# Attention and a Fourier mix on one core: another outermost dimension for two kinds of transfer, and new figures for transfers in the planner

## The chip, the cores and the metric

The kernel runs on one core of a Trainium2 chip. A core has five engines with queues of their own: TensorE (PE, matmuls; its weight loads are shown apart as PEld), VectorE (DVE), ScalarE (ACT), GpSimd (POOL) and SyncE (SP), which here issues every transfer. Sixteen DMA engines move the data. The metric is the device time of one execution in microseconds (us), the median of the runs. All data is float32 and the matmuls take it in the float32r form.

## The reference

Two results stand side by side in the output of 2048 x 2048: attention with 32 heads of 32 channels, and the real part of a two-dimensional Fourier transform made with given matrices.

```python
H = 32; Dh = D // H                       # B, S, D = 1, 2048, 1024
q, k, v = split(x @ wqkv)                 # each (B, H, S, Dh)
scores = einsum("bhqd,bhkd->bhqk", q, k) * Dh ** -0.5
p = softmax(scores, axis=-1)
o = einsum("bhqk,bhkd->bhqd", p, v)
a = o.transpose(0, 2, 1, 3).reshape(B, S, D) @ wo

re = einsum("bsd,ed->bse", x, dft_hid_re)
im = einsum("bsd,ed->bse", x, dft_hid_im)
b = einsum("ts,bse->bte", dft_seq_re, re) - einsum("ts,bse->bte", dft_seq_im, im)
return concatenate([a, b], axis=-1)
```

## The kernel before, in words

**Dense products.** The projections to queries, keys and values (`qkv`), the two Fourier stages (`dense1`, `dense2`) and the output projection (`project`) are done with a scheme of seven products of half-size blocks, whose sums and differences are formed by `fetch` (line 389) on DVE or POOL. Each operand is split into a high and a low part (`halves`, lines 409 to 414), and three matmuls (high x high, low x high, high x low) make one product; line 325 issues them. The text calls these matmuls the fills. Intermediate tensors live in DRAM: `qk_d` for queries and keys, `v_d` for values, `u_d` for partial sums of the seven products, `o_d` for the heads' results, `r_d` for the inverse row sums. Loads of kept partial sums are `c<-u_d` (line 636), and line 557 or 559 adds the result of a group of matmuls to them. In the steps that load and store many `u_d`, from about 540 to 810 us, the queries, keys and values of the later blocks are made.

**Attention** runs beside the fills, head by head. `scores` (line 1062) makes the scores in rows of queries, 1024 keys at a time; DVE takes the maximum (line 1068), ACT the exponentials and their row sums (line 1071). Then `transposed` makes the scores again with keys on the partitions and with the maximum as two more rows of the product (line 1193), so that ACT's exponential (line 1197) is the numerator itself. Line 1211 multiplies it with the values, and lines 1222 and 1224 gather the result in a tile `ot`. Its 128 partitions are 4 groups of 512 queries times 32 channels.

**Row sums.** `sums(h)` turns the row sums of head h, takes the inverse, stores it to `r_d[h]` (8 KB, line 1161) and loads it back into `rt` (line 1154), each group's 512 values onto its 32 partitions. `result(h)` multiplies `ot` with `rt` (line 1239) and stores it to `o_d[h // 4]` (line 1241). `project` reads `o_d` back as operands of 128 rows, four heads times 32 channels for one group of queries, when the heads are done.

**Order.** The program is written out by a planner. Each operation is an `Op` with an engine, a cost in us, what it waits for and a rank; `Plan` keeps a clock for each engine and starts an operation when its engine is free and its inputs are there. PE takes its work from three streams of attention and the list of fills. Some element-wise operations go to POOL or DVE, whichever the plan finds free. Operations of SP cost `ISSUE` each; a transfer of `kb` ends when the bytes ahead of it have moved at `KB_US` = 340 KB per us, and `LANDING` = 1.8 us later; SP begins one only if the plan's backlog of bytes is at most `QUEUE` = 1.0 us. What the plan decides is the fixed order of each engine's instructions. The times at which they run are the chip's.

Of the kernel before, what the change touches and what calls it, by code (L numbers as in the profile page):

```python
# [9 lines left out]
F32 = mybir.dt.float32  # L10
# [7 lines left out]
P = 128  # L18
S = 2048
D = 1024  # L20
H = 32
DH = 32
NC = D // P
NS = S // P
NB = 512
# [9 lines left out]
class Op:  # L35


    __slots__ = ("engine", "cost", "emit", "rank", "kb", "other", "left", "ready", "end", "begun", "then", "soon")

    def __init__(self, engine, cost, emit, rank=0.0, kb=0, other=None):  # L40
        self.engine, self.cost, self.emit, self.rank, self.kb, self.other = engine, cost, emit, rank, kb, other
        self.left, self.ready, self.end, self.begun = 0, -1e3, None, False
        self.then, self.soon = [], []


# [15 lines left out]
class Plan:  # L61
# [13 lines left out]
    def __init__(self):  # L75
        self.now = 0.0
        self.free = {e: 0.0 for e in ("PE", "ACT", "DVE", "POOL", "SP")}
        self.pending = {e: [] for e in ("ACT", "DVE", "POOL", "SP")}
        self.able = {e: [] for e in ("ACT", "DVE", "POOL", "SP")}
        self.dma = 0.0  # L80
        self.seq = 0

    def op(self, engine, cost, emit, after=(), uses=(), rank=0.0, kb=0, order=None, other=None):

        o = Op(engine, cost, emit, rank, kb, other)
        seen = set()
        for d in after:
            if d is not None and id(d) not in seen:  # L90
                seen.add(id(d))
                self._wait(o, d)
        for u in uses:
            u.append(o)
        if order is not None:
            p, order.first = order.first, o
            if p is not None and not p.begun:
                p.soon.append(o)
                o.left += 1
        if o.left == 0:  # L100
            self._release(o)
        return o
# [18 lines left out]
    def start(self, o, e=None):  # L121
        e = e or o.engine
        o.emit(e) if o.other else o.emit()
        o.begun = True
        self.free[e] = self.now + (o.cost if e == o.engine else o.other[1])
        if o.kb:
            self.dma = max(self.dma, self.free[e]) + o.kb / self.KB_US
            o.end = self.dma + self.LANDING
        else:
            o.end = self.free[e]  # L130
            self.free[e] -= self.OVERLAP.get(e, 0.0)
        for t in o.then:
            t.ready = max(t.ready, self.after(o, e, t))
            t.left -= 1
            if t.left == 0:
                self._release(t)
        for t in o.soon:
            t.ready = max(t.ready, self.now)
            t.left -= 1
            if t.left == 0:  # L140
                self._release(t)
        o.then = o.soon = ()
        o.emit = None
# [28 lines left out]

    def begin(self, e):

        return self.free[e] if e != "SP" else max(self.free[e], self.dma - self.QUEUE)


@with_exitstack
def kernel(
# [11 lines left out]
    nc = tc.nc  # L191

    dram = ctx.enter_context(tc.tile_pool(name="dram", bufs=1, space=DRAM))
# [4 lines left out]
    v_d = [dram.tile([P, 16, NS, DH], F32, name=f"v_d{b}") for b in range(2)]  # L198
    r_d = [dram.tile([NS, P], F32, name=f"r_d{h}") for h in range(H)]

    o_d = [dram.tile([4, P, NB], F32, name=f"o_d{c}") for c in range(NC)]
    ab_d = [[[dram.tile([P, NB], F32, name=f"ab_d{m}_{e}_{k}") for k in range(NS)] for e in range(2)] for m in range(2)]
    s1_d = [dram.tile([P, 4, P], F32, name=f"s1_d{i}") for i in range(8)]
    t1_d = [dram.tile([P, NB], F32, name=f"t1_d{n}") for n in range(8)]
# [69 lines left out]
    ES, ET = 1.22, 0.61  # L274
    MAX, EVAC, CAST, BIT = 1.22, 0.69, 0.45, 0.27
    SUB = 1.34
    ISSUE = 0.36

    LATE = 0.3
    HB = 0  # L280
# [13 lines left out]
    op = pl.op  # L294
# [639 lines left out]
    def project():  # L934


        def q_a(r, k, j, c):
            return o_d[4 * k + c][2 * r + j], [o for h in range(4) for o in o_st[16 * k + 4 * c + h]]

        def a_terms(p, j, c):  # L940
            q = lambda r, k: q_a(r, k, j, c)
            return {
                1: lambda: [(1, *q(0, 0))], 2: lambda: [(1, *q(0, 1))], 4: lambda: [(1, A22[j][c])],
                5: lambda: [(1, A22[j][c]), (1, *q(1, 0))],
                6: lambda: [(1, A22[j][c]), (-1, S2[j][c])],
                7: lambda: [(1, *q(0, 0)), (-1, *q(1, 0))],
                3: lambda: [(1, *q(0, 1)), (-1, S2[j][c])],
            }[p]()

        def b_terms(p, c):  # L950
            q = lambda k, e: wo[4 * k + c, :, e * NB : e * NB + NB]
            return {
                1: lambda: [(1, q(0, 0), [])], 2: lambda: [(1, q(1, 0), [])], 3: lambda: [(1, q(1, 1), [])],
                5: lambda: [(1, q(0, 1), []), (-1, q(0, 0), [])],
                6: lambda: [(1, T2[c]), (1, q(0, 0), [])],
                7: lambda: [(1, q(1, 1), []), (-1, q(0, 1), [])],
                4: lambda: [(1, T2[c]), (-1, q(1, 0), [])],
            }[p]()


        WHERE = {
            1: ([16, 20], 0), 7: ([8, 12], 24), 2: ([0, 8], 20), 6: ([12, 0], 24),
            5: ([8, 12], 20), 3: ([0, 8], 24), 4: ([12, 0], 20),
        }
        A, B, X, Y = {}, {}, {}, {}

        def kept(name):
            box = {}

            def get():  # L970
                if "t" not in box:
                    box["t"] = op_pool().tile([P, NB], F32, name=name)
                return box["t"]

            return Kept(get)

        A22 = [[kept(f"a22_{j}_{c}") for c in range(4)] for j in range(2)]
        S2 = [[kept(f"s2_{j}_{c}") for c in range(4)] for j in range(2)]
        T2 = [kept(f"t2_{c}") for c in range(4)]

        def load_b(p):
            for c in range(4):
                B[p, c] = moving(WHERE[p][1] + c, b_terms(p, c), None, T2[c] if p in (6, 7) else None)

        def load_a(p, which):
            for j, c in which:
                if p == 6:
                    fetch([P, NB], [(1, *q_a(1, 1, j, c))], None, A22[j][c])
                A[p, j, c] = moving(WHERE[p][0][j] + c, a_terms(p, j, c), None, S2[j][c] if p in (6, 7) else None)

        J0, J1 = ([(j, c) for c in range(4)] for j in range(2))
        ORDER = (1, 7, 2, 6, 5, 3, 4)
        tail, where[0] = where[0], within
        load_b(1)
        load_a(1, J0 + J1)
        where[0] = tail
        for x, p in enumerate(ORDER):
            for i in range(8):
                j, t = divmod(i, 4)
                if p == 1 and i % 2 == 0:  # L1000
                    X[i // 2] = accs(4 + i // 2)
                if p == 7 and i % 2 == 0:
                    Y[i // 2] = accs(16 + i // 2)
                h = DONE.get(p)
                to = out[(8 * h[0] + i) * P : (8 * h[0] + i) * P + P, h[1] * NB : h[1] * NB + NB] if h else None
                xi, yi = X[i // 2][i % 2], Y[i // 2][i % 2] if Y else None

                group(((((A[p, j, c]), lambda u, t=t: u[:, t * P : t * P + P]), (B[p, c], whole)) for c in range(4)), 4,
                      gather(1, yi, None, None, None, None) if p == 7 else gather(p, xi, yi, None, to, []))
                if p == 6:  # L1010
                    yi.last = add_op(
                        lambda e, xi=xi, yi=yi: (nc.gpsimd if e == "POOL" else nc.vector).tensor_tensor(out=yi.at(), in0=xi.at(), in1=yi.at(), op=ALU.add),
                        [xi.last, yi.last], [xi.users, yi.users], seq())
                if x < 6 and i == 3:
                    n = ORDER[x + 1]
                    load_b(n)
                    if n != 7:
                        load_a(n, J0)
                if x == i == 0:
                    load_a(7, J0 + J1)  # L1020
                if x < 6 and i == 7 and ORDER[x + 1] != 7:
                    load_a(ORDER[x + 1], J1)
# [97 lines left out]
    def sums(h):  # L1120
# [29 lines left out]

        def spread():
            rt[h] = att().tile([P, NB], F32, name="rt", bufs=1)
            r = r_d[h].rearrange("(j a) b -> j (a b)", j=4).rearrange("j (o n) -> j o n", o=1)
            nc.sync.dma_start(rt[h], r.broadcast_to([4, DH, NB]))

        a = op("DVE", 2 * BIT, sub, exps + told, [tuse, suse, nuse], -2)
        b = op("ACT", BIT, ex, [a], [tuse], -2)
# [2 lines left out]
        d = op("DVE", BIT, copy, [m, *sold], [users, srs], -2)  # L1160
        e = op("SP", ISSUE, lambda: nc.sync.dma_start(r_d[h], box["s"]), [d], [srs], -2, 8)
        rold, ruse = rt_r.take()
        g = op("SP", ISSUE, spread, [e, *rold], [ruse], -2, 256)
        rts[h] = (g, ruse)
        return m

# [69 lines left out]
    def result(h, e, po, ouse):  # L1236
# [1 line left out]
        a = add_op(  # L1238
            lambda e: (nc.gpsimd if e == "POOL" else nc.vector).tensor_tensor(out=po["o"], in0=po["o"], in1=rt[h], op=ALU.mult),
            [e, load], [ouse, ruse], -1)  # L1240
        o_st[h].append(op("SP", ISSUE, lambda: nc.sync.dma_start(o_d[h // 4][:, h % 4 * DH : h % 4 * DH + DH, :], po["o"]), [a], [ouse], -2, 256))

    qkv()
    for w in (1, 0):
# [137 lines left out]
```

## Time and profile before

| | |
|---|---|
| median of three runs | 3128.91 us (3128.57 to 3138.54) |
| profiled execution | 3130.3 us, its span 3128.5 us |
| PE busy | 3065.6 us, 98% of the span |
| DVE, ACT, POOL busy | 2501.8, 2305.5, 888.0 us |
| moved by DMA | 567.76 MB, 181 GB/s in the mean |
| mean granted clock of TensorE | 0.995 |

The span is the time from the first to the last instruction of the profiled execution; the execution's own time has 1.8 us more around it. Lines such as "L1241 SPq DMA_DIRECT2D o_d<-ot" name the line of the kernel, the engine's queue, the operation and what it writes and reads. "SPq" is SP's sequencer, the time it needs to issue a transfer. The granted clock is a share of full speed; at 0.5 a matmul takes twice as long.

### The profile page before, as it was taken

To read this page: it belongs to the slowest core of one execution; us is meant where nothing else is said; L and a number is where in the kernel's file an instruction comes from. 1 tells how busy PE (TensorE), PEld (TensorE's weight loads), DVE (VectorE), ACT (ScalarE), POOL (GpSimd) and SP (SyncE) were. 2 spreads that over 40 slices of the span, in tenths; PEclk is the share of its full clock that TensorE was granted. 3 is DMA by queue.
4 is the path that set the end of the run, shared out by engine and by line. 5 is a ranking of instruction groups with operands and counts; after the bars stand their busy time and mean duration, and the time that the engine had idled before them with its cause. 6 is when DMAs were issued, how large, how long until landed. Compare 5 with 4: busy or idle time off the path is not lost.

```text
span 3128.5 us, 45280 instructions
## 1 busy us (share of the span) xinstructions
PE 3065.6 (98%) x15040; PEld 2146.0 (69%) x15040; DVE 2501.8 (80%) x3206; ACT 2305.5 (74%) x4316; POOL 888.0 (28%) x659
## 2 busy tenths in 40 slices
PE   9899999999999999999999999999999999999999
PEld 7687666566666666666666666666666666666787
DVE  7669889977777877787777888888777888887886
ACT  4237888777888888888888887888888878775321
POOL 3423323401102222221001244233211235333453
PEclk9999999999999999999999999999999999999999
DMA  9976557876634544464443576545433467456952
GB/s 332 321 239 189 185 166 239 298 225 191 194 94 145 184 142 148 138 190 146 138 126 100 182 228 194 157 146 181 132 116 103 147 215 227 150 156 194 329 177 92
DMA packets 357368, 567.76 MB, mean 181 GB/s; under 512 B 84336, under 2 KB 85872, under 8 KB 357136
## 3 DMA queue, kind: packets, MB, share of 16 engines
q1 hardware_dynamic: 357136, 564.86, 57.0%
q8 instruction: 121, 1.98, 0.3%
q14 instruction: 111, 0.91, 0.1%
HBM read 407.70 MB, written 156.50 MB: 180 GB/s over the span
## 4 chain that ended last, share of the span: by engine, by line
PE 80%; DVE 11%; DMA 5%; issue 2%; ACT 2%; SPq 1%; POOL 0%; DVEq 0%; ACTq 0%; POOLq 0%
PE pd L325 34%; PE psT L1193 13%; PE pd L1211 13%; PE psS L1062 13%; PE psT L325 5%; DVE negm L1068 3%; ACT psS L1071 1%; DVE slot L414 1%; DMA raw<-in_xa 1%; DVE slot L411 1%; DVE raw L389 1%; DVE h L411 1%; DVE l L414 1%; DMA g<-in_ct 1%; DMA c<-u_d 0%
## 5 line engine op out<-in xcount | busy, mean ns | idle before, releaser
L1197 ACT ACTIVATE pt<-psT 128x512 f32<-128x512 f32 x2048 | 1159.5, 629 | 332.6 <-PE psT L1193 327.5
L1068 DVE TENSOR_REDUCE negm<-psS 128x1 f32<-128x1024 f32 x1024 | 1232.7, 1218 | 194.0 <-PE psS L1062 190.0
L1071 ACT ACTIVATE psS<-psS,negm 128x1024 f32<-128x1024 f32 x1024 | 1148.7, 1122 | 175.7 <-DVE negm L1068 169.5
L325 PE MATMUL pd<-slot,h 128*128 128x512 f32 x3336 | 1163.4, 397 | 9.6 <-DVE c L557 6.2
L1193 PE MATMUL psT<-qs,ks 98*128 98x512 f32 x2048 | 822.7, 405 | 2.3 <-ACT pt L1197 1.2
L325 PEld LDWEIGHTS pd<-slot,h 128*128 128x128 f32 x3336 | 632.8, 190 | 163.0 <-issue 9.3
L325 PE MATMUL pd<-slot,l 128*128 128x512 f32 x1668 | 662.5, 397 | 0.8 <-POOL l L414 0.8
L1193 PEld LDWEIGHTS psT<-qs,ks 98*128 98x128 f32 x2048 | 385.1, 189 | 199.3 <-issue 69.0
L1062 PE MATMUL psS<-ks,qs 96*128 96x512 f32 x1552 | 478.6, 399 | 14.5 <-ACT psS L1071 13.0
L1211 PE MATMUL pd<-pt,vt 128*32 128x512 f32 x4096 | 467.3, 597 | 5.1 <-DVE e L774 1.9
L389 POOL TENSOR_TENSOR raw<-raw,g 128x512 f32<-128x512 f32 x218 | 290.3, 1336 | 555.8 <-DVE raw L389 114.7
L414 POOL TENSOR_TENSOR l<-raw,h 128x512 fp32r<-128x512 f32 x159 | 210.9, 1327 | 792.6 <-DVE h L411 322.6
L325 PEld LDWEIGHTS pd<-slot,l 128*128 128x128 f32 x1668 | 316.7, 190 | 77.5 <-issue 6.3
L1062 PEld LDWEIGHTS psS<-ks,qs 96*128 96x128 f32 x1552 | 288.5, 189 | 98.2 <-ACT psS L1071 32.5
L414 POOL TENSOR_TENSOR slot<-raw,slot 128x512 fp32r<-128x512 f32 x142 | 199.7, 1411 | 418.3 <-DVE slot L411 344.7
L1211 PEld LDWEIGHTS pd<-pt,vt 128*32 128x32 f32 x4096 | 120.2, 110 | 281.2 <-issue 260.8
L1071 ACT ACTIVATION_READ_ACCUMULATOR psS<-psS,negm 128x1 f32 x1024 | 243.9, 238 | 0.0
L325 PE MATMUL pd<-slot,slot 128*128 128x512 f32 x768 | 196.2, 393 | 0.5 <-DVE e L774 0.4
L1224 DVE TENSOR_TENSOR ot<-ot,pd 128x512 f32<-128x512 f32 x96 | 65.9, 687 | 139.1 <-PE pd L1211 138.8
L325 PEld LDWEIGHTS pd<-slot,slot 128*128 128x128 f32 x768 | 144.4, 188 | 33.7 <-DVE e L774 0.8
L389 DVE TENSOR_TENSOR raw<-raw,g 128x512 f32<-128x512 f32 x154 | 129.0, 843 | 35.5 <-DMA raw<-in_ct 10.3
L1062 PE MATMUL psS<-ks,qx 96*128 96x512 f32 x496 | 154.2, 400 | 2.6 <-ACT psS L1071 2.1
(115 smaller groups left out, 2101.4 us busy)
## 6 DMA issues: line engine op xcount, KB each, us to landing
raw<-in_ct SPq DMA_DIRECT2D x224, 256.0 KB
g<-in_ct SPq DMA_DIRECT2D x128, 256.0 KB
c<-u_d SPq DMA_DIRECT2D x104, 256.0 KB
qk_d<-e SPq DMA_DIRECT2D x52, 512.0 KB
qs<-qk_d SPq DMA_DIRECT2D x128, 192.0 KB
ks<-qk_d SPq DMA_DIRECT2D x128, 192.0 KB
raw<-ab_d SPq DMA_DIRECT2D x96, 256.0 KB
g<-ab_d SPq DMA_DIRECT2D x80, 256.0 KB
```

Of the source, the lines that this page charges most:

```text
L325: nc.tensor.matmul(box["ps"], a[1]((a[0].hi, a[0].lo)[u]()), b[1]((b[0].hi, b[0].lo)[v]()), start=k == 0, stop=k == n - 1)
L389: (nc.gpsimd if e == "POOL" else nc.vector).tensor_tensor(out=dest(), in0=dest() if a is None else a.get(), in1=other["q"] if "q" in other ...
L411: nc.vector.tensor_copy(hi(), raw())
L414: (nc.gpsimd if e == "POOL" else nc.vector).tensor_tensor(out=lo(), in0=raw(), in1=f(hi()), op=ALU.subtract)
L1062: nc.tensor.matmul(p[:, i * NB : i * NB + NB], (qx["t"] if own else QS[h % 2][0:96])[:, qt * P : qt * P + P], KS[h % 2][0:96, c * 1024 + i ...
L1068: nc.vector.tensor_reduce(out=ST["negm"][:, c, qt : qt + 1], in_=box["p"], axis=AX.X, op=ALU.max, negate=True)
L1071: nc.scalar.activation(box["p"], box["p"], AF.Exp, bias=ST["negm"][:, c, qt : qt + 1], accum_out=ST["sums"][:, c, qt : qt + 1])
L1193: nc.tensor.matmul(box["p"], KS[h % 2][0:98, t * P : t * P + P], QS[h % 2][0:98, j * NB : j * NB + NB], start=True, stop=True)
L1197: nc.scalar.activation(box["t"], box["p"], AF.Exp)
L1211: nc.tensor.matmul(po["p"][j * DH : j * DH + DH, :], VT[h][:, k, :], box["t"], start=(k == t + 1 - PVB), stop=(k == t), tile_position=(0, ...
L1224: nc.vector.tensor_tensor(out=po["o"], in0=po["o"], in1=po["p"], op=ALU.add)
```

## The change

Two kinds of transfer get another shape. The store of a head's result wrote four blocks of 32 rows, four outermost; `o_d` is now laid out so that it writes 128 rows of 2 KB. The load of the row sums read four rows, each spread over 32 partitions, in one transfer with four outermost; it is now four transfers with 32 rows outermost each. `project` reads the rows of `o_d` in the order channel, head instead of head, channel, and the host lays out `wo` to match. In the plan an issue costs 0.46 instead of 0.36, a ring of eight end times keeps at most eight transfers under way, and an operation of several transfers (`lanes`) counts each of them. The rest of the computation is as before.

```diff
+        self.lane = [0.0] * 8
...
         if o.kb:
-            self.dma = max(self.dma, self.free[e]) + o.kb / self.KB_US
-            o.end = self.dma + self.LANDING
+            for _ in range(o.lanes):
+                t = max(self.free[e], self.lane[0])
+                self.dma = max(self.dma, t) + o.kb / o.lanes / self.KB_US
+                o.end = self.dma + self.LANDING
+                self.lane = self.lane[1:] + [o.end]
+                if o.lanes > 1:
+                    self.free[e] = t + o.cost
...
-        return self.free[e] if e != "SP" else max(self.free[e], self.dma - self.QUEUE)
+        return self.free[e] if e != "SP" else max(self.free[e], self.dma - self.QUEUE, self.lane[0])
...
-    o_d = [dram.tile([4, P, NB], F32, name=f"o_d{c}") for c in range(NC)]
+    o_d = [dram.tile([P, 4, NB], F32, name=f"o_d{c}") for c in range(NC)]
...
-    ISSUE = 0.36
+    ISSUE = 0.46
...
-            return o_d[4 * k + c][2 * r + j], [o for h in range(4) for o in o_st[16 * k + 4 * c + h]]
+            return o_d[4 * k + c][DH * (2 * r + j) : DH * (2 * r + j) + DH].rearrange("d h n -> (d h) n"), [o for h in range(4) for o in o_st[16 * k + 4 * c + h]]
...
-            r = r_d[h].rearrange("(j a) b -> j (a b)", j=4).rearrange("j (o n) -> j o n", o=1)
-            nc.sync.dma_start(rt[h], r.broadcast_to([4, DH, NB]))
+            r = r_d[h].rearrange("(j a) b -> j (a b)", j=4)
+            for j in range(4):
+                nc.sync.dma_start(rt[h][j * DH : j * DH + DH], r[j : j + 1].broadcast_to([DH, NB]))
...
-        g = op("SP", ISSUE, spread, [e, *rold], [ruse], -2, 256)
+        g = op("SP", ISSUE, spread, [e, *rold], [ruse], -2, 256, lanes=4)
...
-        o_st[h].append(op("SP", ISSUE, lambda: nc.sync.dma_start(o_d[h // 4][:, h % 4 * DH : h % 4 * DH + DH, :], po["o"]), [a], [ouse], -2, 256))
+        o_st[h].append(op("SP", ISSUE, lambda: nc.sync.dma_start(o_d[h // 4][:, h % 4, :], po["o"]), [a], [ouse], -2, 256))
...
-        "wo": c(A_wo.reshape(NC, P, D)),
+        "wo": c(A_wo.reshape(NC, 4, DH, D).transpose(0, 2, 1, 3).reshape(NC, P, D)),
```

More of the change, by code (lines that the diff above doesn't have):

```diff
@@ L35 @@
 class Op:
-    __slots__ = ("engine", "cost", "emit", "rank", "kb", "other", "left", "ready", "end", "begun", "then", "soon")
+    __slots__ = ("engine", "cost", "emit", "rank", "kb", "other", "left", "ready", "end", "begun", "then", "soon", "lanes")
     def __init__(self, engine, cost, emit, rank=0.0, kb=0, other=None):
         self.engine, self.cost, self.emit, self.rank, self.kb, self.other = engine, cost, emit, rank, kb, other
-        self.left, self.ready, self.end, self.begun = 0, -1e3, None, False
+        self.left, self.ready, self.end, self.begun, self.lanes = 0, -1e3, None, False, 1
         self.then, self.soon = [], []
@@ L80, in __init__, with op @@
         self.dma = 0.0
+        self.lane = [0.0] * 8
         self.seq = 0
-    def op(self, engine, cost, emit, after=(), uses=(), rank=0.0, kb=0, order=None, other=None):
+    def op(self, engine, cost, emit, after=(), uses=(), rank=0.0, kb=0, order=None, other=None, lanes=1):
         o = Op(engine, cost, emit, rank, kb, other)
+        o.lanes = lanes
         seen = set()
```

## The prediction

> **What bounds the kernel now.** First the page: its span and its engine table.
>
> ```profile
> span 3128.5 us, 45280 instructions
> PE 3065.6 (98%) x15040; PEld 2146.0 (69%) x15040; DVE 2501.8 (80%) x3206; ACT 2305.5 (74%) x4316; POOL 888.0 (28%) x659
> ```
>
> TensorE is the bound, busy 98% of the span. The change leaves its matmuls as they are, so it can only move the 62.9 us in which PE is idle and the stretches in which it runs slow. The view by stretch says where these lie (its columns: start and end, length, busy time and instructions of PE, PEld, DVE, ACT, POOL, then granted clock, DMA share, GB/s).
>
> ```profile
> 0.00:120.00 120.00, 100.39 (x410) 80.02 (x411) 78.06 (x96) 46.72 (x77) 40.39 (x34) 0.94 0.97 323
> 540.00:625.00 85.00, 77.85 (x353) 50.70 (x353) 79.36 (x104) 65.92 (x124) 41.66 (x32) 0.96 0.87 303
> 625.00:720.00 95.00, 87.29 (x412) 57.54 (x411) 63.12 (x81) 70.16 (x132) 6.44 (x5) 0.95 0.75 216
> 720.00:810.00 90.00, 88.27 (x455) 58.49 (x454) 75.98 (x102) 71.91 (x137) 18.25 (x14) 1.00 0.70 226
> 810.00:1800.00 990.00, 989.21 (x5000) 680.36 (x5001) 768.93 (x984) 842.60 (x1598) 194.15 (x149) 1.00 0.47 144
> 1800.00:2900.00 1100.00, 1086.91 (x5466) 739.45 (x5468) 912.36 (x1172) 871.93 (x1647) 355.04 (x264) 1.00 0.54 168
> 2900.00:3128.50 228.50, 221.67 (x977) 179.27 (x969) 179.81 (x225) 51.66 (x84) 92.46 (x60) 1.00 0.58 198
> ```
>
> The start loses 19.6 us and the tail 6.8 us; 810 to 1800 us loses 0.8 us in 990. From 540 to 810 us PE idles 16.6 us, with 0.04 x 85 + 0.05 x 95 = 8.2 us more lost to a lower clock, while DMA is at 0.70 to 0.87. From 1800 to 2900 us it idles 13.1 us. Only these two stages have something for a change of transfers.
>
> Then the chain in order of time, its longest transfers in those stages (start, length):
>
> ```profile
> 617.16 9.17 DMA qx<-qk_d
> 703.84 7.68 DMA c<-u_d
> 796.55 8.11 DMA raw<-in_xb
> 2584.73 7.48 DMA g<-in_ct
> ```
>
> And the instructions of the tiles that the change touches, and of two for comparison (duration on SP's queue, min/median/max), with a stretch around one lone store of a result (start, us, engine):
>
> ```profile
> L1154 SPq DMA_DIRECT2D rt<-r_d x32: 566/580/899, 283.0 to 2834.0; - x32
> L1241 SPq DMA_DIRECT2D o_d<-ot x32: 570/591/604, 353.4 to 2904.8; - x32
> L1161 SPq DMA_DIRECT2D r_d<-rs x32: 318/330/604, 279.9 to 2826.0; - x32
> L1176 SPq DMA_DIRECT2D vt<-v_d x32: 319/327/433, 233.7 to 2738.7; - x32
> 2403.31 0.58 SPq L1241 DMA_DIRECT2D o_d<-ot  x1
> 2405.30 0.33 SPq L373 DMA_DIRECT2D raw<-ab_d  x1
> 2408.10:2410.10 2.00, 2.00 (x10) 1.67 (x9) 1.97 (x4) 2.00 (x5) 0.00 (x0) 1.00 0.20 75
> ```
>
> A store of 256 KB that SP issued at 2403.31 is still moving 5 to 7 us later, at a fifth of the DMA engines' time: four rows outermost occupy about four of sixteen engines. I call it a clog: a transfer issued behind it needs those four engines too and waits. Just before each long transfer of the chain such a one was issued:
>
> ```profile
> 612.98 0.59 SPq L1241 DMA_DIRECT2D o_d<-ot  x1
> 616.48 0.58 SPq L1154 DMA_DIRECT2D rt<-r_d  x1
> 702.57 0.59 SPq L1241 DMA_DIRECT2D o_d<-ot  x1
> 703.22 0.53 SPq L614 DMA_DIRECT2D v_d<-e  x1
> 703.84 5.18 SPq L636 DMA_DIRECT2D c<-u_d  x1
> 712.40 0.58 SPq L1154 DMA_DIRECT2D rt<-r_d  x1
> 2584.05 0.58 SPq L1154 DMA_DIRECT2D rt<-r_d  x1
> ```
>
> **The change, part by part.** *The clogs go.* Both transfers get 128 or 32 rows outermost. What the clogs cost PE now is read around them:
>
> ```profile
> 627.00:640.00 13.00, 9.12 (x47) 3.29 (x46) 10.45 (x14) 7.32 (x14) 1.27 (x1) 0.87 0.89 303
> 702.50:710.00 7.50, 6.52 (x27) 4.57 (x25) 4.03 (x6) 6.91 (x13) 0.00 (x0) 1.00 0.66 145
> 710.00:720.00 10.00, 7.62 (x20) 6.04 (x21) 4.29 (x5) 4.53 (x9) 0.00 (x0) 0.66 0.84 209
> 796.00:811.00 15.00, 13.68 (x74) 8.08 (x73) 12.29 (x17) 10.43 (x22) 3.91 (x4) 1.00 0.90 274
> 2584.00:2606.00 22.00, 20.30 (x102) 13.31 (x101) 18.68 (x19) 17.14 (x34) 14.99 (x12) 1.00 0.84 260
> ```
>
> Around 630 us: 3.88 idle and 0.13 x 13 = 1.69 of clock, 5.6. Around 710 us: 0.98 + 2.38 idle and 0.34 x 10 = 3.4 of clock, 6.8. Around 800 us 1.3, around 2595 us 1.7. Together 15.4 us, the most that this part can give; the least is 0, if the loads behind come late for another reason (in 540 to 810 us DMA has other work for 0.70 to 0.87 of its time). A loss is excluded here: the same bytes go over more engines. I take the first two whole (12.4), because in both the chain runs through the very load issued behind the clog, and half of the others (1.5), where vector work shares the chain: 13.9. Elsewhere the 64 transfers are hidden, for 810 to 1800 us holds a third of them and idles 0.8 us. What is late next at 712 us is the store v_d<-e of line 614, which the code writes in pieces of 32 floats, issued between the clog and the late load; it stays, and the issue of 5.18 us right behind it may be its doing in part.
>
> *Four issues in place of one.* Each head's spread of the row sums becomes four issues at about 0.33 us (the nearest rows are 16 and 128 rows outermost, 330 and 327 ns) for one of 0.58: +0.74 us on SP, 23.7 us in all; the store saves 0.59 - 0.33, 8.3 us in all. Behind them in SP's queue wait the next loads. Between 0 (SP waits for producers anyway) and 15.4 us net I take 1.0, the three extra issues of one head in the dense stage, where SP stood on the chain at 703 us; nothing below 0, for issues are added.
>
> *The rows of the output projection* are read as 128 rows of 2 KB, as now; with the weights rearranged on the host this costs nothing.
>
> *The plan.* 0.46 for an issue instead of 0.36, and at most eight transfers under way, change no work but its order. The trace has four issues back to back in 1.84 us, 0.46 each, so the new figure is the truer one:
>
> ```profile
> 595.81 1.84 SPq L249 DMA_DIRECT2D qs<-qk_d  x4
> L414 POOL TENSOR_TENSOR l<-raw,h 128x512 fp32r<-128x512 f32 x159 | 210.9, 1327 | 792.6 <-DVE h L411 322.6 <-PE psT L1193 207.1 <-PE pd L325 164.9
> L414 DVE TENSOR_TENSOR l<-raw,h 128x512 fp32r<-128x512 f32 x162 | 131.4, 811 | 4.8 <-ACT h L409 0.2
> L325 PE MATMUL pd<-slot,l 128*128 128x512 f32 x1668 | 662.5, 397 | 0.8 <-POOL l L414 0.8
> 594.00:607.00 13.00, 9.43 (x30) 6.33 (x32) 10.22 (x15) 6.59 (x13) 2.35 (x3) 0.74 0.70 237
> ```
>
> In the built programs the first 784 matmuls and 238 SP issues stand as before, so the start keeps its loss. Later, the fills stand up to 21 matmuls ahead of their old place against the heads, and near the end up to 24 behind; in the dense stage the u_d loads stand some two places earlier in SP's queue and the loads of queries and keys three to four later. 24 element-wise operations move from DVE to POOL. Each takes 1327 - 811 = 0.52 us longer there: 12.4 us if all were exposed, nothing if as now (0.8 us of waits for POOL in 1668 matmuls). It also frees 24 x 0.81 = 19 us of DVE, which is no bound at 80%. I take 0, because the row of waits is the thing itself. The new order may also lose or cure the third stall of the dense stage, 594 to 607 us, which has no clog before it: 3.57 idle and 0.26 x 13 = 3.4 of clock, 7.0. I take 0 and keep it for the range.
>
> *Sum.* -13.9 + 1.0 = -12.9. The profiled execution took 3130.3 us, 1.8 around its span, and stands 1.4 over the median of the runs, 3128.9: 3117.4 on it, 3116 for the median.
>
> **A rule on the clock.** The row 594 to 607 us has a clock of 0.74 after PE had waited 2.2 us, and 627 to 640 us 0.87 after waits none of which exceeded 1.3 us:
>
> ```profile
> 597.01 0.80 PE L325 MATMUL pd<-slot,h 128*128 128x512 f32 x1 [2.23 <-DVE c L557]
> 634.18 4.96 PE L1211 MATMUL pd<-pt,vt 128*32 128x512 f32 x32 [1.30 <-DVE c L557]
> ```
>
> The Trainium skill ("TensorE: Matmul & The Clock Gate", "Why this matters for your kernels") has the clock halve after about 3 us of idleness. By that rule the first two stalls, if they only shrank to half, would give back all their clock time and half their idleness, 5.1 + 3.6 = 8.7 us; the trace does not agree with it, for it lost clock after shorter waits. By the rows a stall cut to half may keep its clock price, and the first two would then give only (3.88 + 3.36) / 2 = 3.6 us, which is the value used below.
>
> **Rivals.** *Hidden, or only halved.* The loads stay late because bytes, not clogs, fill the stage (0.87 and 303 GB/s at 540 to 625 us), or the stalls shrink by half as just priced: 3122 to 3128, within 0.3%. A variant is that only the store's clog goes, and the four 64 KB parts of the row sums take as long together as the one transfer did. Both kinds stand before or in the first two places, so half of their 12.4 goes, 6.2: 3123. The Trainium skill ("DMA: Bandwidth & Descriptors", rules for kernel authors) speaks for it: split halves serialize, and transfers of 64 KB and less are mostly overhead; no row here shows such a part. Against the variant: r_d<-rs has only 16 rows outermost, and it issues as fast as a transfer with 128, not like one with four. That the limit of eight does nothing is likely in itself, since the plan already issues only at a backlog under 1 us; then 0.46 alone reorders.
>
> *Slower.* The dense stage has three stalls of 7.0, 5.6 and 6.8 us, mean 6.5. Queries and keys that stand three to four places later, each place 0.46 us, hold up the heads just where DMA is fullest, and each late load costs such a stall. With five stalls (from 4.5 on it decides) the stage loses 32.3 in place of 19.4: 3142. For it: 0.87 DMA share. Against: the loads that PE waits for there, the u_d ones, come earlier.
>
> *More.* All 15.4 go, the 594 us stall too, and a third of the 11.4 us that 1800 to 2900 us idles besides: 15.4 + 7.0 + 3.8 = 26: 3103.
>
> **How the numbers follow.** Under 0.3% (9.4 us) a run of this kernel can hardly be told from no change. Forecast 0.41 (3110 to 3119.5), more 0.13, hidden or halved 0.29, slower 0.17. Faster by over 0.3%: 0.54; within: 0.29; slower: 0.17. The range 3101 to 3141 reaches to 3103 and to the edge of 3142 and leaves out about one in ten.
>
> **What would show it.** Right: issues of rt and o_d at about 0.33 us; no transfer over 6 us on the chain behind them; PE idle from 540 to 810 us down from 16.6 to about 8 and its clock there near 0.99. Wrong: transfers of 7 us and more still behind rt; PE waiting for u_d loads, queries or keys at new places; more than 0.8 us of idleness in 810 to 1800 us, or waits for POOL in the matmuls, which only the new order could bring.

## The result, and the profile after

The changed kernel takes 3121.1 us in the median of 13 runs (3119.3 to 3122.0), the kernel before 3128.9 (3125.5 to 3138.5): 0.9971 of it, 95% interval 0.9963 to 0.9980. In a second comparison the ratio was 0.9963 (0.9951 to 0.9976). The forecast was 3116; the gain is real (both intervals end below 1) and lies at the edge of the 0.3% that the prediction called the limit of what can be told.

The tiles of the change in the profile after (duration on SP's queue, min/median/max; under each the time from issue to landing of all transfers of that tile's name, which the profile now gives):

```profile
L1162 SPq DMA_DIRECT2D rt<-r_d x128: 302/413/1085, 279.7 to 2827.3; - x128
DMA to landing us min/median/max: 1.9/2.8/5.2
L1249 SPq DMA_DIRECT2D o_d<-ot x32: 319/326/724, 351.8 to 2895.4; - x32
DMA to landing us min/median/max: 2.0/4.0/5.6
```

A store of a result now lands after 4.0 us in the median (the row under the tile ot); before, one was still moving 6.8 us after its issue. It issues in 0.33 us instead of 0.59; a part of the row sums issues in 0.41, not the 0.33 that was assumed. By stretch (columns as in the prediction):

```profile
540.00:625.00 85.00, 75.86 (x344) 49.90 (x345) 75.22 (x101) 61.15 (x115) 38.17 (x28) 0.94 0.88 295
625.00:720.00 95.00, 92.58 (x459) 59.71 (x458) 67.36 (x85) 75.11 (x143) 10.73 (x9) 0.96 0.79 232
720.00:810.00 90.00, 89.73 (x446) 61.58 (x446) 77.28 (x104) 75.57 (x145) 25.26 (x19) 1.00 0.70 234
810.00:1800.00 990.00, 986.50 (x4993) 678.01 (x4996) 774.14 (x977) 837.00 (x1593) 199.13 (x152) 1.00 0.46 143
1800.00:2900.00 1100.00, 1091.15 (x5495) 743.47 (x5485) 910.37 (x1161) 867.71 (x1641) 378.62 (x280) 1.00 0.54 169
```

From 540 to 810 us PE idles 11.8 us instead of 16.6, and loses 8.9 us to the clock instead of 8.2. From 1800 to 2900 us it idles 8.9 instead of 13.1. From 810 to 1800 us it idles 3.5 instead of 0.8. Each stretch is read from one execution. Two of the changed kernel (after and after_pair) differ in idleness by at most 0.4 us in the stages from 540 to 1800 us and by 1.4 us from 1800 to 2900 us. The chain's long transfers are gone: the longest after 200 us that its view lists is this one.

```profile
1419.66 5.44 DMA raw<-in_xb
```

### The profile page after: what moved, and what is told of

It is laid out like the page before. It is cut to its first block, busy times and chain, and to the rows that moved or that the text cites. A ratio compares the mean times of both kernels' runs of the same rounds, so it can differ in the third digit from the quotient of the medians.

```text
span 3119.8 us, 45400 instructions
## 1 busy us (share of the span) xinstructions
PE 3066.8 (98%) x15040; PEld 2151.0 (69%) x15040; DVE 2503.5 (80%) x3182; ACT 2299.1 (74%) x4316; POOL 924.9 (30%) x683
## 4 chain that ended last, share of the span: by engine, by line
PE 66%; DVE 6%; ACT 1%; issue 1%; DMA 0%; POOL 0%; SPq 0%; ACTq 0%; DVEq 0%; POOLq 0%
PE pd L332 29%; PE psT L1201 12%; PE pd L1219 11%; PE psS L1069 11%; PE psT L332 3%; DVE negm L1075 2%; ACT psS L1078 1%; DVE raw L396 1%; DVE h L418 1%; DVE slot L421 1%; DVE l L421 0%; DVE slot L770 0%; DVE slot L418 0%; DVE e L781 0%; PE psS L1152 0%
## 5 line engine op out<-in xcount | busy, mean ns | idle before, releaser
L1069 PE MATMUL psS<-ks,qs 96*128 96x512 f32 x1552 | 479.0, 399 | 12.1 <-ACT psS L1078 11.1
L421 POOL TENSOR_TENSOR l<-raw,h 128x512 fp32r<-128x512 f32 x174 | 233.1, 1339 | 798.5 <-DVE h L418 407.7
L396 POOL TENSOR_TENSOR raw<-raw,g 128x512 f32<-128x512 f32 x229 | 307.9, 1348 | 422.6 <-DVE raw L396 102.4
L421 POOL TENSOR_TENSOR slot<-raw,slot 128x512 fp32r<-128x512 f32 x131 | 182.2, 1396 | 396.6 <-DVE slot L418 319.0
L418 DVE CAST h<-raw 128x512 fp32r<-128x512 f32 x305 | 153.4, 503 | 15.8 <-PE pd L332 13.8
L421 DVE TENSOR_TENSOR slot<-raw,slot 128x512 fp32r<-128x512 f32 x153 | 156.4, 1025 | 6.0 <-ACT slot L416 2.4
```

What stands on the lines that cost most here:

```text
L418: nc.vector.tensor_copy(hi(), raw())
L1069: nc.tensor.matmul(p[:, i * NB : i * NB + NB], (qx["t"] if own else QS[h % 2][0:96])[:, qt * P : qt * P + P], KS[h % 2][0:96, c * 1024 + i ...
```

## The experiments

### The layouts and the order, apart

The first pair: the new layouts in the old order of every engine, and the old layouts in the new order. The excerpts show the lines that tell the runs apart; `project`, the store and `wo` always follow the shape of `o_d`.

```diff
 # layout_only: the kernel before, with
+    o_d = [dram.tile([P, 4, NB], F32, name=f"o_d{c}") for c in range(NC)]
...
+            for j in range(4):
+                nc.sync.dma_start(rt[h][j * DH : j * DH + DH], r[j : j + 1].broadcast_to([DH, NB]))
...
 # order_only: the changed kernel (lanes=4 and 0.46 stay in the plan), with
+    o_d = [dram.tile([4, P, NB], F32, name=f"o_d{c}") for c in range(NC)]
...
+            nc.sync.dma_start(rt[h], r.broadcast_to([4, DH, NB]))
```

> Old order of every engine, both transfers with 128 or 32 rows outermost. Clog theory: the whole gain and more of it, 3128.9 - 8 to 3128.9 - 13, 3116 to 3121; PE idle from 540 to 810 us falls from 16.6 us to about 8, the waits at 628 to 634 us and at 712 us go. Order theory (the new order made the gain): 3128.9, no change over 2 us. Halved theory: 3123 to 3125.

> Order of the changed kernel on every engine, both transfers with four outermost as before. Clog theory: no gain, 3126 to 3134, with transfers of 6 us and more behind rt and o_d; a loss of some us would mean that the new order costs something that the layout hides. Order theory: the whole gain, 3121.

Measured: layout_only 3118.6 us where the kernel before took 3130.4, 0.9958 (0.9945 to 0.9971). order_only 3130.8, 0.9997 (0.9988 to 1.0006). The layouts give the whole gain, the new order nothing. Three transfers of the chain of order_only stand behind old-shaped ones as before, issued 1.6, 2.2 and 1.7 us ahead of them:

```profile
2575.48 8.85 DMA g<-ab_d
2653.55 7.18 DMA g<-ab_d
2834.80 8.99 DMA raw<-in_ct
```

Where the 12 us came from, layout_only tells by the prediction's own stretches:

```profile
540.00:625.00 85.00, 78.28 (x350) 48.86 (x349) 80.18 (x104) 65.06 (x122) 40.46 (x31) 0.96 0.90 305
625.00:720.00 95.00, 91.01 (x457) 58.94 (x456) 69.04 (x89) 73.28 (x140) 6.43 (x5) 0.98 0.77 230
720.00:810.00 90.00, 89.86 (x449) 62.62 (x448) 77.56 (x105) 77.58 (x148) 20.82 (x16) 1.00 0.69 232
1800.00:2900.00 1100.00, 1090.28 (x5481) 745.62 (x5480) 916.79 (x1180) 866.88 (x1636) 353.82 (x263) 1.00 0.53 170
627.00:640.00 13.00, 10.20 (x51) 4.03 (x51) 11.39 (x14) 7.30 (x14) 1.27 (x1) 0.87 0.80 284
702.50:710.00 7.50, 7.50 (x34) 6.01 (x33) 5.79 (x6) 6.71 (x14) 0.00 (x0) 1.00 0.93 203
710.00:720.00 10.00, 9.28 (x56) 5.16 (x55) 7.73 (x11) 6.51 (x13) 0.00 (x0) 1.00 0.93 256
```

Around 710 us the idleness falls from 3.36 to 0.72 us and the clock is whole: 6.0 of the 6.8 us are back. Around 630 us hardly anything is: 2.80 idle where 3.88 was, and the clock at 0.87 as before, 1.1 of 5.6. From 720 to 810 us 1.6 us are back, from 1800 to 2900 us 3.4. From 540 to 810 us PE idles 10.9 us, where about 8 were expected, and the waits around 630 us, which were to go, are still there.

What holds PE around 630 us without any clog is in its own order of time (start, us, and in brackets the wait):

```profile
628.90 0.73 PE L1062 MATMUL psS<-ks,qs 96*128 96x512 f32 x2 [0.73 <-ACT psS L1071]
630.79 0.73 PE L1062 MATMUL psS<-ks,qs 96*128 96x512 f32 x2 [1.15 <-ACT psS L1071]
632.25 0.99 PE L1062 MATMUL psS<-ks,qs 96*128 96x512 f32 x2 [0.73 <-ACT psS L1071]
633.43 4.87 PE L1212 MATMUL pd<-pt,vt 128*32 128x512 f32 x32 [0.19 <-DVE c L557]
```

Pairs of row scores stand one after the other with nothing between, and each waits for ACT to free one of two buffers. In the kernel before the last row had a wait of 1.30 us for the partial sum, here 0.19: that was the clogs' share.

### One layout at a time

```diff
 # od_only: the kernel before, with
+    o_d = [dram.tile([P, 4, NB], F32, name=f"o_d{c}") for c in range(NC)]
...
 # rt_only: the kernel before, with
+            for j in range(4):
+                nc.sync.dma_start(rt[h][j * DH : j * DH + DH], r[j : j + 1].broadcast_to([DH, NB]))
```

> Old order, only the store of the heads' results has 128 rows outermost. Clog theory: about half of what layout_only gives, 4 to 7 us; the wait at 712 us, behind a store, goes, that at 628 us shrinks. If the row sums' transfer is the only one that matters: 0.

> Old order, only the row sums' transfer is split into four of 32 rows. Clog theory: about half of what layout_only gives, 4 to 6 us; the wait at 628 us shrinks, that at 712 us stays. Theory that four parts of 64 KB serialize and gain nothing: 0, with the chain's transfers behind rt as long as before.

Measured: od_only 3125.1, 0.9982 (0.9973 to 0.9990), 5.4 us; rt_only 3122.6, 0.9971 (0.9960 to 0.9982), 7.8 us. Together 13.2, about what both give at once. Around 710 us two clogs stand one behind the other. In the kernel before, PE waits 3.29 us at 712.38 us, and that wait is the store's: rt_only still has it, low clock and all. od_only keeps its clock there but still idles 3.25 us. First two rows rt_only, then od_only:

```profile
702.50:710.00 7.50, 5.37 (x24) 4.04 (x22) 3.02 (x3) 6.07 (x13) 0.00 (x0) 1.00 0.51 110
710.00:720.00 10.00, 7.72 (x21) 6.17 (x22) 4.46 (x5) 4.67 (x9) 0.00 (x0) 0.66 0.74 215
```

```profile
702.50:710.00 7.50, 6.87 (x30) 5.28 (x29) 4.67 (x5) 6.77 (x13) 0.00 (x0) 1.00 0.86 210
710.00:720.00 10.00, 7.38 (x49) 3.64 (x48) 6.73 (x10) 4.59 (x11) 0.00 (x0) 1.00 0.81 216
```

Most of what is left in od_only belongs to the row sums' transfer, which comes next and has its old shape there. The load of partial sums behind it takes 6.42 us on the chain and holds PE for 2.62 us (rows of SP, of the chain and of PE):

```profile
705.80 0.60 SPq L1154 DMA_DIRECT2D rt<-r_d  x1
706.45 6.42 DMA c<-u_d
714.42 3.64 PE L1211 MATMUL pd<-pt,vt 128*32 128x512 f32 x32 [2.62 <-DVE c L557]
```

With both layouts new, 0.72 us of idleness are left. The clog also holds SP: the issue of the load behind the store took 5.18 us in the kernel before and takes 6.38 in rt_only, but 2.58 in od_only and 2.62 in layout_only (rows of rt_only and layout_only):

```profile
702.49 6.38 SPq L636 DMA_DIRECT2D c<-u_d  x1
701.35 2.62 SPq L636 DMA_DIRECT2D c<-u_d  x1
```

The store v_d<-e of line 614, which the prediction suspected, stands between the two in all four runs; at most the 2.6 us that remain can be its doing. The theory that four parts gain nothing over one transfer falls. The wait around 628 us, which was to shrink, hardly does in rt_only: PE idles 3.06 us from 627 to 640 us, where it idled 3.88.

### Does the order cost anything, and does 0.46 matter?

The changed kernel and layout_only again, on one chip, and the changed kernel with two other figures for an issue.

```diff
-    ISSUE = 0.46
+    ISSUE = 0.41          # issue41; 0.52 in issue52
```

> The changed kernel once more, beside layout_pair on one chip. If the new order costs what the first figures say: 2.5 us slower than layout_pair. If the order costs nothing: within 1 us of it, both near 0.9965 of the kernel before.

> The new layouts in the old order once more, beside after_pair on one chip. Order costs something: 11 to 13 us under the kernel before. Order costs nothing: 8 to 10 us under it, as after_pair.

> The changed kernel with 0.41 for an issue in the plan instead of 0.46: the same work in another order. If the orders are as good as random, the times with 0.36 (layout_pair, old order), 0.41, 0.46 and 0.52 lie within some 5 us without a trend. If the truer figure makes a better order, 0.46 is the fastest and 0.41 lies between 0.36 and 0.46.

> The changed kernel with 0.52 for an issue in the plan. Random orders: within 5 us of the others, either way. Truer figure, better order: slower than after_pair by 1 us or more.

Measured, beside 3132.7 for the kernel before: after_pair 3121.1, 0.9963 (0.9951 to 0.9976); layout_pair 3120.7, 0.9960 (0.9947 to 0.9973); issue41 3118.7, 0.9958 (0.9944 to 0.9971); issue52 3119.4, 0.9961 (0.9948 to 0.9973). Four orders of the same work lie within 2.4 us, without a trend over 0.41, 0.46 and 0.52. With five executions each, the intervals are as wide as those differences. The 2.5 us by which the changed kernel seemed to trail layout_only did not come back; both lie 11.6 to 12.0 us under the kernel before, more than the 8 to 10 expected. The limit of eight does nothing at all: built without it, the changed kernel has the same instructions in the same order on every engine.

### Where a clog costs

New layouts, in the old order, for heads 0 to 7 alone or for heads 8 to 31 alone; and a further clog per head in the changed kernel.

```diff
 # early_heads; late_heads has h >= 8 and c >= 2. project reads an old-shaped o_d in the order channel, head
+    o_d = [dram.tile([P, 4, NB] if c < 2 else [4, P, NB], F32, name=f"o_d{c}") for c in range(NC)]
...
+            if not h < 8:
+                nc.sync.dma_start(rt[h], r.rearrange("j (o n) -> j o n", o=1).broadcast_to([4, DH, NB]))
+                return
...
 # more_clogs
-            nc.sync.dma_start(VT[h], v_d[h // 16][:, h % 16])
+            nc.sync.dma_start(VT[h], v_d[h // 16].rearrange("(p j) a t d -> j p a t d", j=4)[:, :, h % 16])
```

> Old order; new layouts for heads 0 to 7 alone, whose transfers fall before about 950 us. If the clogs cost PE time only where DMA is nearly full (540 to 810 us, heads 3 to 5): 7 to 9 of the 10 to 12 us that the layouts give, 3122 to 3124 where the kernel before takes 3130 to 3132. If each clog costs the same wherever it is: a quarter, about 3 us.

> Old order; new layouts for heads 8 to 31 alone. Clogs cost only where DMA is nearly full: 2 to 4 us, from 1800 to 2900 us. The same wherever: three quarters, about 8 us.

> The changed kernel with one more transfer per head of four outermost, the load of the values (its rows come in another order, so that the heads' result is another; the work is the same). Clog theory: 32 transfers of one kind, as in od_only or rt_only, give back 5 to 8 us of the gain: 3126 to 3129, with transfers behind vt of 6 us and more. If the gain came from anything else in the new layouts: no change, 3121.

Measured, beside 3131.1 for the kernel before: early_heads 3125.5, 0.9978 (0.9970 to 0.9987). By the ratio that is 6.9 us for 16 transfers, 0.43 us each; by the medians 5.6 us, a little under the 7 to 9 expected. late_heads 3127.5, 0.9987 (0.9979 to 0.9996): 4.1 us by the ratio for 48 transfers, 0.09 us each; 3.7 by the medians. The sum, 11.0 or 9.3 us, is about that of both layouts everywhere. By the ratios a clog costs some five times as much in the first quarter, which holds the dense stage. The intervals give 0.25 to 0.59 us against 0.03 to 0.14, so the difference is clear and the factor is not. The profiles show the places: early_heads gains from 625 to 810 us, late_heads from 1800 to 2900 us, where the kernel before idles 7.71, 1.73 and 13.09 us (first two rows early_heads, the third late_heads):

```profile
625.00:720.00 95.00, 89.77 (x444) 58.41 (x446) 67.14 (x86) 73.73 (x138) 6.82 (x6) 0.98 0.77 228
720.00:810.00 90.00, 89.86 (x456) 61.69 (x449) 78.52 (x107) 75.25 (x144) 19.00 (x15) 1.00 0.71 235
1800.00:2900.00 1100.00, 1090.54 (x5492) 741.70 (x5491) 913.84 (x1174) 871.69 (x1648) 356.18 (x264) 1.00 0.54 169
```

The profiled execution of early_heads is its slowest, 3130.4 us, so its stretches tell the place and not the size. more_clogs: 3132.3 us, 1.0001 (0.9993 to 1.0010); 32 transfers of the same bytes with four rows outermost take the whole gain back, some 11 us, 0.35 us each, where 5 to 8 us were expected. Its stretches show where:

```profile
625.00:720.00 95.00, 89.95 (x442) 58.50 (x444) 65.77 (x83) 74.09 (x139) 10.01 (x8) 0.96 0.80 227
810.00:1800.00 990.00, 983.63 (x4970) 673.67 (x4969) 771.41 (x973) 833.88 (x1586) 195.27 (x149) 1.00 0.46 142
1800.00:2900.00 1100.00, 1087.53 (x5448) 740.54 (x5448) 908.78 (x1153) 874.46 (x1654) 377.66 (x280) 1.00 0.54 167
```

And a row of its chain (start, length):

```profile
1833.32 9.45 DMA vt<-v_d
```

PE idles 2.6, 2.9 and 3.6 us more than in the changed kernel in these three, and the values' load itself is on the chain with 9.45 us. No wait of PE that the profile lists names this load, and what follows it on the chain is vector work that does not read it. So why these 32 cost more than the 32 of od_only or rt_only stays open.

### A fourth buffer

```diff
-    CR = Ring(3)
+    CR = Ring(4)          # and four tiles c; NPT = 18, Ring(8) in behind()
```

> New layouts, old plan figures, and four buffers in place of three for the kept partial sums (tile c), paid for with one of 19 buffers of the numerators and one of nine in the tail. If the stalls left at 595 to 635 us are loads of partial sums that wait for a buffer: 3 to 7 us under layout_pair. If they are set by the order of PE and DVE: no change.

Measured: 3117.4 us, 0.9950 (0.9937 to 0.9963), the lowest ratio of all, with an interval that overlaps those of layout_only and, at its edge, of the changed kernel. The stalls were not removed:

```profile
540.00:625.00 85.00, 74.05 (x332) 46.07 (x331) 78.02 (x101) 59.49 (x111) 38.31 (x29) 0.92 0.89 302
625.00:720.00 95.00, 94.46 (x478) 64.45 (x480) 67.75 (x90) 76.95 (x145) 9.05 (x7) 1.00 0.84 250
```

Idleness of 10.95 us and a clock of 0.92 before 625 us, then almost none: they moved to an earlier time. The edit changes buffers, ring sizes and with them the order, so whether the fourth buffer as such helps stays open.

## Why the prediction was right or wrong

**The mechanism** was right and shown from both sides: taking the clogs away in the old order gives 12 us, adding 32 others takes some 11 us away again, and the order alone gives nothing. How a clog holds the load behind it is known in part. That the load waits for the same four engines was argued from a DMA share of 0.20; that SP is held as well, for 5 to 6 us in place of 2.6, is measured. No run separates the two.

**The clogs' term.** "I take the first two whole (12.4)" is the step that failed in part. The place at 710 us gave 6.0 of 6.8. The place at 630 us gave 1.1 of 5.6: the chain did run through a load behind a clog, but it joins PE's work at one point only, and most of PE's idle time in that window, 2.58 of 3.88 us, was three waits for score buffers (0.70, 1.18 and 0.70), which stood in the profile beside the one for the load. "Half of the others (1.5)" was too low: 720 to 810 us and 1800 to 2900 us gave 1.6 + 3.4 = 5.0. So these places measured 6.0 + 1.1 + 5.0 = 12.1 where 13.9 was put: two wrong sizes nearly cancel, and that is luck. (From 810 to 1800 us layout_only idles 1.0 us more than the kernel before.) The prediction's list of the longest transfers in its two stages also left out two, issued just behind clogs (a store of a result at 1910.26 us, a load of row sums at 1924.19 us):

```profile
1911.50 6.79 DMA g<-in_ct
1925.59 8.49 DMA raw<-ab_d
```

They cost little: from 1890 to 1945 us PE idles 2.90 us in the kernel before and 2.36 in layout_only. Late heads give 4.1 us; "elsewhere the 64 transfers are hidden" was too strong, though 810 to 1800 us had indeed nothing to give.

**The issues.** 0.33 us for a part was put, 0.41 measured; the prediction's own row of four issues back to back, 0.46 each, was nearer. What the issues cost in time was not measured by itself; the 1.0 us stays an estimate.

**The plan.** The change of order was taken at 0, and order_only gives 0.9997. That the limit of eight does nothing was said and is so. That 24 operations on POOL cost nothing is only consistent with this: no run moved them alone.

**The size.** 12.9 us were forecast. The layouts in the old order measure 11.8 and 12.0 against the medians beside them; the change itself 7.8 in the first comparison and 11.6 in the second, whose intervals overlap, about 0.2 to 0.5%. The first figure, 3121.1, lies between the forecast's band (to 3119.5) and that of "halved" (from 3122). Whether the gain is over or under 0.3% these intervals do not settle.

**The rivals.** "Halved" was near the first figure, but not for its reasons: bytes did not take the place of the clogs, and the four parts of the row sums, of 64 KB each, gain 7.8 us over the one transfer (rt_only). What was cited against such parts does not hold here. "Slower" had its five stalls nowhere: in the changed kernel the heads wait at another place instead, while the stall at 712 us is gone. A row of PE's order of time in the changed kernel (in brackets the wait):

```profile
608.38 0.50 PE L1201 MATMUL psT<-qs,ks 98*128 98x512 f32 x1 [3.55 <-ACT pt L1205]
```

That is one wait of 3.55 us for ACT to free a score buffer, not for a load of queries or keys. ACT had waited 2.64 us for a maximum, which DVE reached only after casts and splits that stand ahead of it. order_only waits 3.54 us at the same place, so it comes with the order and not with the layouts. "More" did not happen.

**What would show it.** PE's idleness from 540 to 810 us was to fall to 8 us and its clock to 0.99. It fell to 11.8, and the clock did not rise: the new order has a stall of its own at 608 us, with a clock of 0.72 from 607 to 613 us, and the one around 630 us stays, with 0.74 from 627 to 640 us. One sign of being wrong came too: from 810 to 1800 us PE idles 3.5 us instead of 0.8. order_only has 2.9 us there and layout_only 1.8, so most of it comes with the order, to which the prediction had put down all of it. Over the whole run the new stalls are no dearer than the old ones.

## What to carry to other kernels

Here a transfer with four rows outermost was slow and held up what was queued behind it, and the price was paid there. So look for a small outermost count on transfers that no engine waits for, too, above all where DMA is as busy as in the dense stage here (a share of 0.70 to 0.87). When the chain names a late load, check in PE's own order what PE waits for in that window before giving the load the whole window. A planner's figure that is truer need not make a faster program; run two or three values before crediting one.

## What was not expected of the hardware

Issuing one transfer with four rows outermost takes SP 0.58 us, and 0.33 us with 128: the worse shape is also the slower to issue. And the clock was lost after short waits: in layout_only 0.87 from 627 to 640 us after waits of 0.73, 1.15 and 0.73 us one after the other, which adds to the prediction's row of 1.30 us. The length of one wait does not settle it: in od_only PE waits 2.62 us at 714 us, longer than any of these and than the 2.23 us of the stretch at 594 us, and the clock is 1.00 from 710 to 735 us.
